# Attention and highway layer in one kernel: the weights come in as bf16 by four GpSimd DMAs

## The chip, the cores and the metric

The kernel runs on one core of a Trainium2 chip. The metric is the device time of one execution in microseconds (us), the median of three runs. The profile is of one further execution; its times count from the start of that execution's span.

TensorE (PE) multiplies matrices, VectorE (DVE), ScalarE (ACT) and GpSimd (POOL) work element by element, and SyncE (SP) here does nothing but issue DMAs. Each engine takes its instructions in one fixed order. Only PE does matrix products[...].

## The reference

The input is `q`, `k`, `v` of (4 batches, 8 heads, 768 positions, 64 columns) in float32. The attention is linear with a decay `lam` per head, in blocks of 64 positions:

```python
intra = (qb @ kb.T * Dmask) @ vb            # within the block
inter = (qb * lam**(pos+1)) @ kv_state      # what came before
out   = intra + inter
kv_state = lam**64 * kv_state + (kb * lam**(63-pos)).T @ vb
```

The result, rearranged to `x` of 3072 tokens by 512 columns, goes through a highway layer with two 512 x 512 weights:

```python
H = relu(x @ w_h);  T = sigmoid(x @ w_t + b_t)
result = T * H + (1 - T) * x                # = x + T * (H - x)
```

## The kernel before, in words

The work is cut into 12 chunks of 256 positions, three per batch. Each chunk has all 8 heads, and two halves of 128 tokens. The numbers behind a name below are the chunk and the part: `k1.0` is the first four heads of `k` of chunk 1 (chunks 0 and 1 come in two parts each, the others whole).

For each chunk:

- `load` (line 208) fetches `q`, `k`, `v` with DMAs of 256 KB on SP's queue, in rows of 512 bytes; whole chunks take two DMAs for each of the three.
- `cast_k` makes `k` bf16 (its copy runs in line 173 on ACT, 175 on DVE and POOL); `scale` (line 217) multiplies `q` and `v` by powers of `lam` and writes bf16.
- `trans` (line 223) transposes `k` and `q` on PE, and `evac_h` copies the result out of PSUM.
- `scores` (line 239), `mask` (line 243, DVE), and `intra` (line 264) are the product inside the block; `state` (line 272) adds to the running `kv` sum in PSUM, an evacuation to `ss` copies it out, and `inter` (line 252) multiplies with it. `inter` and `intra` of a chunk add up in PSUM tile `o`, which `evac_x` copies to `xT`.
- `block` (line 293) is the highway product: `ffn h g0.0` is half the columns of `xT @ w_h` for chunk 0 in eight matmuls, `ffn t g0.0` the same with `w_t`. `hmx` (297), `sigm` (306) and `thmx` (309) make the elementwise part; `turn` (315) transposes back and adds; `evac_o` copies out; `store` (line 324) writes to memory on SP's queue.

Line 198 is `fill`: matmuls of an identity at the start whose results nobody uses, which keep PE busy while the first data comes.

The weights: `load_w` (line 169) issues eight DMAs of 256 KB on SP, each of half the rows and half the columns of one weight, in rows of 1 KB, into float32 tiles `w_f`. Eight casts (`cw`) then make bf16 tiles `w_b`: four on POOL, three on ACT, one on DVE. `wh.y0` below stands for the first 256 columns of `w_h`, `wt.y1` for the last 256 of `w_t`.

The order is not left to a scheduler. Every step is a task with a number. The list `ORDER` says in which order tasks are emitted, and so the order of each engine's queue, the SP queue of DMAs among them. The strings in `EN` say which engine takes a task that could run on several (`A` for ACT, `V` for DVE, `G` for POOL). Waits between engines follow from the tiles that are read and written.

The start, decoded from `ORDER` (fills left out):

```
SP   v0.0 k0.0 q0.0 q0.1 k0.1 v0.1 q1.0 k1.0 k1.1 q1.1 v1.0 v1.1 q2 k2 v2
     wt.y1 (2 DMAs) wh.y0 (2) wh.y1 (2) wt.y0 (2) q3 k3 v3 ...
POOL scale v0.1, q1.0; cast k1.0; scale q1.1, q2, v2;
     cast wh.y0, wh.y1, wt.y0 (2); th g0.1 ...
PE   trans k0.0 q0.0 q0.1 k0.1, scores 0.0 0.1, trans k1.0 q1.0, intra 0, state 0.0, inter 0,
     state 0.1, scores 1.0, trans q1.1, state 1.0, trans k1.1, state 1.1, inter 1, scores 1.1,
     trans k2, trans q2, intra 1, scores 2.0, state 2.0, ffn t g0.1, ffn t g1.1,
     inter 2, scores 2.1, ffn h g0.0, ...
```

Of the kernel before, what the change touches and what calls it, by code (L numbers as in the profile page):

```python
# [8 lines left out]
F32 = mybir.dt.float32  # L9
# [11 lines left out]
class Task:  # L21
# [9 lines left out]


LETTER = dict(A="ACT", V="DVE", G="POOL")
KINDS = {"SP": "lw l l2 st st1 st3", "DVE": "m hx hx1 hx4 thD thD1 thD4 btc", "POOL": "thP thP1 thP4", "ACT": "g g1 g4 pow tab", "PE": "bt fill tr tr2 kv i i0 s a f f1 f4 x x1 x3"}
FIXED = {kind: eng for eng, kinds in KINDS.items() for kind in kinds.split()}
LA = 5
XB = 3
# [4 lines left out]
TH = ["DVE", "POOL"]  # L42
GROUPS = [[0], [1], [2], [3], [4], [5], [6], [7], [8], [9], [10]]
EN = dict(
    cw="GVGGGAAA", ck2="VVGA", cq2="VVGG", cv2="VGVV", et2="VAAVAVAV", ss="AAVAAAAVAVAAAAVVAVAV", xT="VAVAAAAAAAAAAAAAAAAAAAAA",
    eo="AVVAAAVAAVAVAVAAAAVAVA", ck="VAAGGAGVGG", cq="GVGGGGGGGG", cv="GGGGGGGGGG", et="AVAVAVVAVAAAAAAAAAAA", eo1="A", eo3="AA")
ORDER = [
    34, 32, 20, 33, 21, 43, 22, 42, 23, 16, 44, 24, 25, 26, 83, 27, 35, 17, 28, 82, 37, 29, 30, 36, 92, 31, 46, 38, 40, 93, 39,
    41, 84, 45, 50, 48, 51, 47, 52, 94, 49, 53, 86, 55, 133, 54, 56, 85, 132, 57, 88, 95, 134, 90, 18, 89, 58, 91, 96, 12, 59, 19,
    64, 60, 63, 87, 61, 107, 65, 100, 97, 14, 62, 108, 102, 98, 109, 99, 136, 103, 0, 101, 104, 105, 106, 110, 135, 2, 111, 138,  # L50
    8, 140, 112, 139, 10, 137, 141, 113, 6, 13, 4, 114, 15, 145, 142, 171, 146, 115, 1, 73, 147, 143, 170, 123, 3, 74, 172, 9,
    144, 211, 124, 148, 66, 149, 7, 11, 150, 71, 5, 210, 67, 68, 72, 116, 174, 69, 212, 151, 121, 70, 152, 117, 75, 251, 173, 178,
    122, 118, 153, 179, 176, 175, 119, 250, 154, 177, 120, 79, 76, 155, 214, 252, 185, 77, 80, 180, 161, 181, 186, 184, 213, 187,
    125, 289, 188, 182, 218, 189, 162, 156, 190, 183, 215, 219, 288, 216, 157, 159, 217, 158, 191, 254, 290, 160, 220, 192, 225,
    126, 221, 193, 226, 129, 253, 201, 227, 328, 127, 130, 258, 163, 256, 202, 194, 329, 257, 255, 259, 224, 195, 228, 263, 222,
    330, 229, 196, 292, 223, 230, 260, 264, 197, 231, 370, 164, 261, 291, 232, 265, 167, 233, 199, 198, 165, 293, 369, 262, 168,
    200, 266, 294, 267, 296, 331, 203, 295, 234, 407, 297, 236, 268, 332, 235, 298, 368, 237, 269, 303, 334, 299, 238, 270, 241,
    333, 304, 406, 271, 239, 305, 335, 336, 240, 242, 373, 204, 408, 300, 205, 337, 302, 306, 272, 307, 301, 243, 448, 308, 207,
    338, 273, 372, 208, 343, 309, 344, 339, 447, 277, 310, 345, 311, 274, 410, 278, 446, 279, 275, 244, 371, 280, 276, 319, 487,
    245, 409, 342, 320, 346, 281, 340, 374, 347, 341, 488, 376, 348, 411, 375, 317, 377, 312, 486, 412, 313, 247, 413, 349, 318,  # L60
    450, 81, 378, 248, 381, 350, 314, 379, 351, 382, 414, 449, 315, 206, 383, 352, 415, 451, 316, 282, 380, 353, 283, 249, 384,
    452, 385, 321, 454, 453, 386, 285, 416, 284, 490, 286, 387, 455, 169, 421, 417, 354, 422, 388, 287, 389, 423, 357, 489, 246,
    355, 128, 359, 491, 358, 209, 390, 356, 360, 78, 494, 391, 166, 361, 420, 495, 424, 131, 418, 322, 425, 419, 397, 426, 325,
    323, 492, 398, 326, 324, 362, 427, 327, 493, 456, 461, 395, 457, 428, 462, 429, 365, 463, 363, 460, 396, 366, 364, 464, 458,
    465, 499, 367, 392, 459, 466, 435, 500, 393, 501, 430, 394, 496, 431, 399, 467, 432, 436, 468, 497, 469, 437, 433, 498, 438,
    434, 502, 400, 503, 439, 472, 401, 504, 470, 402, 473, 403, 471, 505, 404, 474, 440, 506, 405, 477, 441, 520, 475, 442, 478,
    507, 476, 443, 509, 508, 479, 444, 512, 510, 521, 445, 513, 514, 511, 523, 522, 515, 480, 483, 524, 516, 481, 528, 484, 526,
    525, 482, 529, 531, 485, 527, 517, 532, 530, 518, 533, 534, 519, 535, 536]


@with_exitstack
def kernel(
# [11 lines left out]
    nc = tc.nc  # L84
# [4 lines left out]
    DM = H * D  # L89
    KC = DM // 128  # L90
# [4 lines left out]
    singles = ctx.enter_context(tc.tile_pool(name="singles", bufs=1))  # L95
# [32 lines left out]
    id_f = singles.tile([KC, KC], F32)  # L128
    nc.vector.tensor_copy(id_f, id128[0:KC, 0:KC])
    bt_col = singles.tile([128, KC], F32)  # L130
    w_f = [singles.tile([128, KC, DM], F32, name=f"w_f{i}") for i in range(2)]
    w_b = [singles.tile([128, KC, DM], BF16, name=f"w_b{i}") for i in range(2)]
    wh, wt = w_b

# [16 lines left out]
    def task(kind, emit, reads=(), writes=(), after=(), only=()):  # L151
        eng = FIXED.get(kind)
        if eng is None:
            i = count.get(kind, 0)
            count[kind] = i + 1
            eng = LETTER[EN[kind][i]]
        t = Task(kind, eng, emit, [made[x] for x in reads], [made[x] for x in writes], after, only)
        tasks.append(t)
        return t

    V, A, P, T = nc.vector, nc.scalar, nc.gpsimd, nc.tensor
    ENG = {"DVE": V, "POOL": P}


    def piece(x, y, i):
        return x[:, 2 * i:2 * i + 2, y * 256:(y + 1) * 256]

    def load_w(w, y, i):
        nc.sync.dma_start(out=piece(w_f[w], y, i), in_=piece((moe_w_h, moe_w_t)[w].rearrange("(kc p) n -> p kc n", p=128), y, i))

    def copy(eng, dst, src):
        if eng == "ACT":
            A.activation(dst, src, AF.Copy)  # L173
        else:
            ENG[eng].tensor_copy(dst, src)  # L175

    w_done = {}
    for y, w in ((0, 0), (0, 1), (1, 0), (1, 1)):
        w_done[w, y] = []
        for i in range(2):  # L180
            a = task("lw", lambda eng, w=w, y=y, i=i: load_w(w, y, i))
            w_done[w, y].append(task("cw", lambda eng, w=w, y=y, i=i: copy(eng, piece(w_b[w], y, i), piece(w_f[w], y, i)), after=[a]))


    def powers(eng):
# [98 lines left out]
    def group(n, b):  # L284
        for g in GROUPS:
            if n in g:
                return g[0], 2 * (n - g[0]) + b, 2 * len(g)
        return n + b, 0, 1
# [39 lines left out]
    for n in range(N):  # L328
        bt, c = divmod(n, NST)
        P2 = n < PARTS  # L330
        parts = [slice(0, 4), slice(4, 8)] if P2 else [slice(0, 8)]
        y = "2" if P2 else ""
# [58 lines left out]
        for b in range(2):  # L391
            g, r, z = group(n, b)
            y = {1: "1", 2: "", 4: "4"}[z]
# [9 lines left out]
            w = 1 if z == 4 else 2  # L403
# [24 lines left out]
            y = "3" if fin else "1"  # L428
# [45 lines left out]
```

## Time and profile before

| | |
|---|---|
| time, median of 3 runs | 113.19 us (113.16 to 113.62) |
| span of the profiled execution | 110.9 us |
| PE busy | 101.5 us (92%) |
| DVE, ACT, POOL busy | 78.4, 72.9, 63.5 us |
| DMA | 27.57 MB, 20.98 MB read and 6.29 MB written in main memory, 249 GB/s over the span |
| casts of the weights | 4 on POOL of 614 ns, 3 on ACT of 623 ns, 1 on DVE of 416 ns |

How to read it: the page gives the busy share of each engine in 40 slices of the span (one slice is 2.8 us here), a digit for each, nine for 90% or more. `PEclk` is PE's granted clock in tenths of full speed. The chain is the work that ended last, followed back step by step to what released each. A line such as "20.64 1.90 PE w L223 x16" is a start, a length, an engine, the tile written, the source line and the number of instructions.

### The profile page before, as it was taken

How to read it: one execution, taken by the hardware profiler on the slowest of the kernel's cores; microseconds unless marked ns; L12 is line 12 of the kernel's file. 1: busy time of each engine (PE TensorE's matmuls, PEld its weight loads, DVE VectorE, ACT ScalarE, POOL GpSimd, SP SyncE). 2: the span in 40 equal slices, each digit the busy share in tenths (PEclk: the TensorE clock that was granted, in tenths of full speed). 3: DMA queues.
4: the chain of work that ended last, by engine and by line, in shares of the span. 5: the costliest groups of instructions: out<-in, count | busy, mean ns of one | idle time of the engine just before them, and what ended most of it. 6: DMA issues, size and time to landing. Idle time of an engine off the chain costs nothing.

```text
span 110.9 us, 4776 instructions
## 1 busy us (share of the span) xinstructions
PE 101.5 (92%) x2073; PEld 86.3 (78%) x2073; DVE 78.4 (71%) x128; ACT 72.9 (66%) x137; POOL 63.5 (57%) x55
## 2 busy tenths in 40 slices
PE   4996489689999999999999999999999999999960
PEld 1353469578889889888888889999899888889950
DVE  0179896684998899797778854788775797764630
ACT  3574443177288967668695788787878844785780
POOL 6004626263469899988979979899940040401420
PEclk9999965559999999999999999999999999999998
DMA  0999999999999999999999999999995250024263
GB/s 10 267 292 290 290 293 287 293 356 320 253 290 297 288 292 292 290 294 289 293 287 287 279 292 295 292 264 370 392 343 204 107 188 0 6 101 183 101 236 142
DMA packets 43964, 27.57 MB, mean 249 GB/s; under 512 B 1828, under 2 KB 41000, under 8 KB 43944
## 3 DMA queue, kind: packets, MB, share of 16 engines
q1 hardware_dynamic: 43792, 27.27, 88.3%
q8 instruction: 16, 0.26, 1.0%
q14 instruction: 4, 0.03, 0.1%
q10 hardware_dynamic: 152, 0.01, 0.1%
HBM read 20.98 MB, written 6.29 MB: 246 GB/s over the span
## 4 chain that ended last, share of the span: by engine, by line
PE 76%; SPq 11%; DMA 6%; DVE 2%; issue 1%; POOLq 1%; ACT 0%; DVEq 0%
PE w L293 39%; SPq L208 11%; PE w L315 10%; PE w L223 10%; DMA kf<-in_k_dram 6%; PE w L239 5%; PE o L264 5%; PE kv L272 4%; PE o L252 4%; DVE qT L175 1%; POOLq L469 1%; DVE kb L175 1%; DVE hmx L297 0%; ACT o_sb L173 0%; DVEq L175 0%
## 5 line engine op out<-in xcount | busy, mean ns | idle before, releaser
L293 PE MATMUL w<-xT,w_b 128*128 128x256 bf16 (+1 forms) x416 | 46.9, 265 | 0.0
L293 PEld LDWEIGHTS <-w_b 128*128 128x128 bf16 x416 | 36.5, 98 | 4.4
L243 DVE TENSOR_TENSOR m<-w,tri 128x512 bf16<-128x512 f32 x48 | 30.8, 684 | 4.2 <-PE w L239 3.8
L309 POOL TENSOR_TENSOR th<-t_sb,hmx 128x512 bf16<-128x512 bf16 (+1 forms) x13 | 15.1, 1165 | 23.5 <-DVE hmx L297 14.4
L217 POOL TENSOR_TENSOR vs<-vf,pow_k 128x1024 bf16<-128x1024 f32 (+1 forms) x11 | 20.1, 1824 | 12.2 <-DMA vf<-in_v_dram 11.1
L297 DVE SCALAR_TENSOR_TENSOR hmx<-w,xT 128x512 bf16<-128x512 f32 (+1 forms) x26 | 16.5, 646 | 7.7 <-PE w L293 7.4
L217 POOL TENSOR_TENSOR qb<-qf,pow_q 128x1024 bf16<-128x1024 f32 (+1 forms) x11 | 19.2, 1746 | 4.2 <-DMA qf<-in_q_dram 4.2
L306 ACT ACTIVATE w<-w,bt_col 128x256 f32<-128x256 f32 (+1 forms) x26 | 11.2, 432 | 7.6 <-PE w L293 5.7
L173 ACT ACTIVATE xT<-o 128x512 bf16<-128x512 f32 x22 | 12.1, 597 | 3.7 <-PE o L264 2.3
L173 ACT ACTIVATE kT<-w 128x1024 bf16<-128x1024 bf16 (+1 forms) x11 | 10.0, 906 | 6.9 <-PE w L223 6.9
L315 PE MATMUL w<-id,th 128*128 128x128 bf16 x96 | 12.9, 219 | 0.6 <-POOL th L309 0.6
L239 PE MATMUL w<-qT,kT 64*64 64x128 bf16 x384 | 12.8, 231 | 0.7 <-ACT kT L173 0.3
L315 PE MATMUL w<-id,xT 128*128 128x128 bf16 x96 | 12.9, 220 | 0.0
L173 ACT ACTIVATE o_sb<-w 128x512 f32<-128x512 f32 (+1 forms) x17 | 9.6, 575 | 4.8 <-PE w L315 4.6
L306 ACT ACTIVATE t_sb<-w,bt_col 128x256 bf16<-128x256 f32 (+1 forms) x26 | 10.5, 458 | 3.0 <-PE w L293 3.0
L309 DVE TENSOR_TENSOR th<-w,hmx 128x512 bf16<-128x512 f32 (+1 forms) x13 | 8.4, 648 | 4.2 <-ACT w L306 4.0
L223 PE MATMUL w<-id,kb 128*128 128x128 bf16 x96 | 8.5, 231 | 2.8 <-DVE kb L175 1.4
L272 PE MATMUL kv<-vs,kb 64*64 64x64 bf16 x320 | 10.4, 203 | 0.1
L315 PEld LDWEIGHTS <-th 128*128 128x128 bf16 x96 | 9.4, 98 | 0.9 <-POOL th L309 0.8
L239 PEld LDWEIGHTS <-kT 64*64 64x64 bf16 x384 | 9.1, 112 | 1.2 <-ACT kT L173 0.5
L272 PEld LDWEIGHTS <-kb 64*64 64x64 bf16 x320 | 8.8, 117 | 1.3 <-issue 1.0
L315 PEld LDWEIGHTS <-xT 128*128 128x128 bf16 x96 | 9.3, 98 | 0.5
(46 smaller groups left out, 118.9 us busy)
## 6 DMA issues: line engine op xcount, KB each, us to landing
vf<-in_v_dram SPq DMA_DIRECT2D x24, 256.0 KB, 5.4
kf<-in_k_dram SPq DMA_DIRECT2D x24, 256.0 KB, 5.5
qf<-in_q_dram SPq DMA_DIRECT2D x24, 256.0 KB, 5.5
out_dram<-o_sb SPq DMA_DIRECT2D x23, 256.0 KB, 3.5
w_f<-in_moe_w_t_dram SPq DMA_DIRECT2D x4, 256.0 KB, 6.1
w_f<-in_moe_w_h_dram SPq DMA_DIRECT2D x4, 256.0 KB, 6.2
out_dram<-o_sb SPq DMA_DIRECT2D x2, 128.0 KB, 1.9
lam_bc<-in_lam_dram ACTq DMA_DIRECT2D x1, 4.0 KB, 3.5
```

What stands on the lines that cost most here:

```text
L173: A.activation(dst, src, AF.Copy)
L208: nc.sync.dma_start(out=get(x, n, p)[:, h - hs.start:h - hs.start + 4, :], in_=src[b, h:h + 4, c * 2 * C:(c + 1) * 2 * C, :].rearrange("h ...
L217: ENG[eng].tensor_tensor(dst[:, hs], in0=get(x, n, p).rearrange("p h (j d) -> p h j d", j=J), in1=pw[:, :, :, None].to_broadcast([128, hs. ...
L223: T.transpose(get(x + "tr", n, p)[:, i, j, :], get(x + "b", n)[:, j, h:h + 2, :], id128)
L239: T.matmul(get("s", n, u, e)[half(b), i, j, :], lhsT=turned("k", n)[half(e), hp, b * C + j:(b + 1) * C:J], rhs=turned("q", n)[half(e), hp, ...
L243: V.tensor_tensor(get("m", n, u)[:, e], in0=get("s", n, u, e), in1=tri[:, None].to_broadcast([128, 2, J, C]), op=ALU.mult)
L272: T.matmul(get("kv", n // NST)[half(e), hp, :], lhsT=get("kb", n)[half(b), j, 2 * hp + e, :], rhs=get("vs", n)[half(b), 2 * hp + e, j, :], ...
L293: T.matmul(get(x, g, js[0])[:, i, :], lhsT=w[:, kc, j * 128:(j + 1) * 128], rhs=get("xT", g)[:, kc, :], start=(kc == 0), stop=(kc == KC - 1))
L297: V.scalar_tensor_tensor(get("hmx", g, js[0]), in0=get("h", g, js[0]), scalar=0.0, in1=get("xT", g)[:, js[0]:js[-1] + 1, :], op0=ALU.max, ...
L306: A.activation(get(*gate(g, js))[:, i, :], get("t", g, js[0])[:, i, :], AF.Sigmoid, bias=bt_col[:, j:j + 1])
L309: ENG[TH[js[0] // len(js) % 2]].tensor_tensor(get("th", g)[:, js[0]:js[-1] + 1, :], in0=get(*gate(g, js)), in1=get("hmx", g, js[0]), op=AL ...
L315: T.matmul(get("x", n, b, p)[:, (j - js[0]) * 128:(j - js[0] + 1) * 128], lhsT=get(x, g)[:, j, r * C:(r + 1) * C], rhs=id128, start=(j == ...
```

## The change

The weights no longer come as float32. GpSimd issues four DMAs, one for each weight and half of its columns, which convert to bf16 on the way and write `w_b` directly. So the float32 tiles `w_f` and the eight casts are gone, and SP issues no weight DMA. The purpose is to take the casts off POOL, ACT and DVE, and the weight DMAs out of SP's queue. The number of tasks falls from 537 to 529, and the whole order and the engine choices are planned anew.

```diff
-KINDS = {"SP": "lw l l2 st st1 st3", ... "POOL": "thP thP1 thP4", ...
+KINDS = {"SP": "lw l l2 st st1 st3", ... "POOL": "gw thP thP1 thP4", ...
-    cw="GVGGGAAA", ck2="VVGA", cq2="VVGG", cv2="VGVV", et2="VAAVAVAV", ...
+    ck2="AVGV", cq2="GVGG", cv2="GGGG", et2="AVAAVAAA", ...
-    w_f = [singles.tile([128, KC, DM], F32, name=f"w_f{i}") for i in range(2)]
-    def piece(x, y, i):
-        return x[:, 2 * i:2 * i + 2, y * 256:(y + 1) * 256]
-
-    def load_w(w, y, i):
-        nc.sync.dma_start(out=piece(w_f[w], y, i), in_=piece((moe_w_h, moe_w_t)[w].rearrange("(kc p) n -> p kc n", p=128), y, i))
+    def load_w(w, y):
+        nc.gpsimd.dma_start(out=w_b[w][:, :, y * 256:(y + 1) * 256],
+                            in_=(moe_w_h, moe_w_t)[w].rearrange("(kc p) n -> p kc n", p=128)[:, :, y * 256:(y + 1) * 256])
-        w_done[w, y] = []
-        for i in range(2):
-            a = task("lw", lambda eng, w=w, y=y, i=i: load_w(w, y, i))
-            w_done[w, y].append(task("cw", lambda eng, w=w, y=y, i=i: copy(eng, piece(w_b[w], y, i), piece(w_f[w], y, i)), after=[a]))
+        a = task("gw", lambda eng, w=w, y=y: load_w(w, y))
+        w_done[w, y] = [task("lw", lambda eng: None, after=[a])]
```

The `lw` tasks that remain emit nothing; they only hold a place in the order. The new start, decoded from the new `ORDER` and `EN` (fills left out):

```
SP   q0.0 v0.0 v0.1 k0.0 k0.1 q0.1 q1.0 q2 k1.0 k1.1 q1.1 v1.0 v1.1 k2 v2 q3 k3 v3 ...
POOL DMA wh.y0, DMA wt.y1, DMA wt.y0, scale q0.0, v0.0, v0.1, DMA wh.y1,
     scale q1.0, q2; cast k1.0; scale q1.1, v1.0, v1.1, v2, q3; th g0.1 ...
ACT  cast k0.0 ... cast k2 ...
PE   trans q0.0 k0.0, scores 0.0, trans k0.1 q0.1 q1.0, scores 0.1, intra 0, trans q2,
     state 0.0, trans k1.0, inter 0, trans q1.1, scores 1.0, state 0.1, trans k1.1,
     state 1.0, inter 1, scores 1.1, trans k2, state 1.1, intra 1, ffn h g0.0, scores 2.0,
     state 2.0, ffn h g1.0, ffn h g0.1, inter 2, scores 2.1, ffn t g1.0, ...
```

POOL's queue begins, before and after, with the masks and index tables of the setup.

## The prediction

> **What bounds the kernel now.** I read three things in order: the slices of the page, the stretches of time, then the chain that ended last. From the page:
>
> ```profile
> PE   4996489689999999999999999999999999999960
> PEclk9999965559999999999999999999999999999998
> DMA  0999999999999999999999999999995250024263
> ```
>
> DMA is full from the second slice (2.8 us) to about 83 us; PE is full from the tenth (25 us) to the 38th. So there are two regimes, with the border near 25 us. The stretches show it in numbers (busy time of PE, PEld, DVE, ACT, POOL, then clock, DMA share, GB/s):
>
> ```profile
> 10.00:15.00 5.00, 2.72 (x101) 2.24 (x102) 4.47 (x9) 2.10 (x4) 3.48 (x4) 0.95 1.22 290
> 15.00:20.00 5.00, 4.68 (x109) 3.87 (x102) 3.25 (x7) 1.85 (x4) 1.90 (x1) 0.50 1.15 294
> 20.00:25.00 5.00, 4.04 (x82) 3.65 (x83) 4.09 (x6) 2.64 (x5) 2.40 (x2) 0.53 1.02 326
> 30.00:80.00 50.00, 50.00 (x1127) 44.25 (x1125) 40.33 (x63) 38.95 (x69) 45.43 (x29) 1.00 1.12 298
> 80.00:106.00 26.00, 26.00 (x546) 23.56 (x544) 18.08 (x31) 17.95 (x39) 5.67 (x6) 1.00 0.37 137
> ```
>
> From 30 to 106 us PE has no idle time, at full clock. DVE, ACT and POOL have slack there. Before 25 us PE has idle time and half a clock. The chain says what it waits for:
>
> ```profile
> 13.23 6.57 DMA kf<-in_k_dram
> ...
> 19.89 0.70 DVE kb L175
> ...
> 20.64 1.90 PE w L223 x16
> ...
> 22.56 1.24 DVE qT L175
> ...
> 23.84 0.63 PE w L239 x13
> 24.48 0.39 PE kv L272 x13
> 24.87 1.85 PE w L293 x16
> ```
>
> The DMA is the one of k of chunk 2, 16th of the 256 KB loads on SP, landed at 19.84. The first highway product starts at 24.87, and PE never stops again. So the time is: the moment when the unbroken stretch begins, plus PE work that is still to be done, plus a tail of some 5 us after the last products. Removing work from DVE, ACT or POOL after 25 us shortens none of the three.
>
> The casts and the arrival of the weights, on POOL:
>
> ```profile
> 21.58 1.90 POOL L217 TENSOR_TENSOR vs<-vf,pow_k 128x1024 bf16<-128x1024 f32 x1 [2.63 <-DMA vf<-in_v_dram]
> 24.51 0.61 POOL L175 CAST w_b<-w_f 128x512 bf16<-128x512 f32 x1 [1.02 <-DMA w_f<-in_moe_w_h_dram]
> 25.99 0.61 POOL L175 CAST w_b<-w_f 128x512 bf16<-128x512 f32 x1 [0.87 <-DMA w_f<-in_moe_w_h_dram]
> 27.50 1.38 POOL L175 CAST w_b<-w_f 128x512 bf16<-128x512 f32 x2 [0.89 <-DMA w_f<-in_moe_w_t_dram]
> ```
>
> Each waits for a weight DMA: the third, fifth and seventh of the eight. They are 1.49 and 1.51 us apart for two, so one 256 KB weight DMA occupies the DMA engines for 0.75 us. The v of chunk 2, last of 18 loads, landed at 21.58, before the weights. The weights arrive just in time: each cast is over before PE comes to its block, since PE shows no wait after 25 us.
>
> **What the Trainium skill says.** The page "DMA: Bandwidth & Descriptors", section "Issuing engines are not separate DMA queues", says that DMAs from all issuers run on the same 16 DMA engines and interleave. Its section "Queues, rings and completion order" says that an engine goes round robin between the rings that have work, at packet granularity. The trace before has nearly all bytes on one ring, so it does not show the sharing; it does show the engines full. The same page, "SWDGE vs HWDGE vs iDMA", says a cast in a DMA has to be issued from GpSimd, whose cores write the descriptors in software; no run here shows its cost yet. "TensorE: Matmul & The Clock Gate", section "What's actually happening", says the clock is halved after an idle window and comes back after some 3.4 us of sustained work. The trace agrees on the direction (0.50 from 15 to about 24.6 us, full after 25 us), though PE was 94% busy from 15 to 20 us and stayed at half.
>
> **The change part by part.**
>
> *Casts removed.* On POOL 4 x 0.614 = 2.5 us, ACT 3 x 0.623 = 1.9 us, DVE 0.42 us. All ran between 22.7 and 28.9 us and no PE step waited for them. Worth nothing on the path.
>
> *Weight bytes.* Main memory still gives 2.1 MB of float32; only the SBUF side halves. If reading sets the price, the DMA time is unchanged, 8 x 0.745 = 6.0 us. Bounds: half of that if written bytes counted, twice if the conversion is slow. I take 6.0.
>
> *When the weights come.* This is the part that counts. POOL's setup ends at 2.75 us with an iota, and its next three instructions are three of the four weight DMAs; the fourth follows scale v0.1. SP has then issued only some five loads, and the DMA engines are full from 2.8 us. So all 6.0 us of weights go ahead of, or between, the loads of chunks 0 to 2, where before they came behind all of them. The engines do not idle, so whichever ring goes first, the sum by the landing of k2 is 16 loads plus 8 weight units: 19.84 + 6.0 = 25.8 us. By the same count v1.1, now the 14th load instead of the 12th (q2 was moved ahead of k1), lands two loads earlier, 2 x 0.91, at 24.0. The 0.91 is from the trace: POOL and DVE stop waiting for q2 (14th) at 17.05 and for q0.1 (fourth) at 7.92.
>
> *What hangs on them.* In PE's new order the first highway product, ffn h g0.0, stands behind inter 1, scores 1.1, trans k2, state 1.1 and intra 1. Although its weights are there early, PE can't reach it sooner. From v1.1 at 24.0: scale v1.1 on POOL 1.04, to 25.1; state 1.0 0.5, to 25.6; ss on DVE 0.42, to 26.0; inter 1 0.7 and scores 1.1 0.6 at half clock, to 27.4; two masks 1.29, to 28.7; intra 1 1.07, to 29.8. From k2 at 25.8: cast on ACT 1.05, trans k2 0.9 behind scores 1.1; it fits within. At full clock the four PE steps take half, and intra 1 ends near 28.5. So ffn starts at 28.5 to 29.8 instead of 24.87: +3.7 to +4.9 us.
>
> *Work left at that point.* Before, scores 2.0 and state 2.0 were already done; now they follow: about 0.25 each at full clock, +0.5. I count 46 changes between 64-row and 128-row products on PE after the first highway product, against 42; the chain shows 0.98 against 0.87 us for eight L293 products behind such a change, so 4 x 0.11 = +0.4.
>
> *Descriptors on POOL.* The trace has none. From below take the 0.5 us that SP needs for one unhindered load; from above 3 us, as POOL's work up to scale v1.1 is 9.8 us (seven scales of 1.04, one of 1.90, one cast of 0.61), which fits before 25 us unless the three DMAs take over 9 us. Nothing on the path for anything in these bounds. The scale waits behind them are for data that lands after 5 us anyway.
>
> *The new engine choices and the steady part.* PE is the bound there, and its products are the same in number. I take zero.
>
> Sum: 113.2 + 3.7 to 4.9 + 0.5 + 0.4 gives 117.8 to 119.0. I take 117.9, the lower end, because two rings at work may raise the rate a little (the page has up to 392 GB/s in a slice, against some 290 here).
>
> **The rivals.**
>
> *The weights ride along for nothing.* For it: 290 GB/s with 512-byte rows is not the most that the page shows (392 in a slice with stores), so a second ring might use what the first leaves. Against it: the DMA engines' share is at or above 1. Then k2 lands at 19.84; its chain is cast 1.05, trans 1.0, state 0.6, intra 1.07, so ffn at 23.6, 1.2 us sooner; less 0.5 and 0.4 that is -0.3: 112.9, and 112.5 without the changes on PE. Even this best case gains little. Faster than before.
>
> *Partly hidden.* Half of the 6 us is absorbed: about 115.3.
>
> *The converting DMA is the bound.* Conversion at half rate makes 12 us of the 6, or descriptors cost 4 us or more each on POOL and push v1.1 to 28.5. k2 at 31.8 gives 113.2 + 6 + 4.9 = 124; the POOL case, 3.4 more than my forecast, 121.5.
>
> **How the numbers follow.** Forecast 0.62, partly hidden 0.14, for nothing 0.14, converting DMA or POOL the bound 0.10. The range: the for-nothing case lies between 112.5 and 113.2 and I leave out its faster half; from above I include the POOL case but not the 124. So 112.9 to 121.5. Chances: faster by over 0.5% 0.10 (the for-nothing case, and gains from the new plan that I don't see), within 0.5% 0.07, slower 0.83.
>
> **What would show it.** Right: k's cast of chunk 2 waits for its DMA until about 25 us, the first L293 product starts at 28 to 30 us, and from there PE is full to some 5 us before the end, with a stretch as long as now plus about 1 us. DMA stays full at about 300 GB/s, and the POOL casts of w_b are gone with no gain for PE. Wrong: GB/s clearly above 330 between 4 and 15 us with k2 near 20 us (for nothing), or scale q0.0 on POOL starting after 12 us with data long there (descriptors), or the first L293 product early but PE with holes after it.

## The result and the profile after

The kernel with the change takes 120.11 us (the median; 119.2 to 120.51) against 113.19 us: a ratio of 1.059, with a 95% interval of 1.052 to 1.066. It is slower, by 6.9 us; the forecast was 117.9, in a range of 112.9 to 121.5. A median counts every execution of a kernel, a ratio leaves out those that came out more than 1.5% above the kernel's fastest. The span of its profiled execution is 118.2 us, against 110.9. Line numbers are those of before less five: the highway products of L293 are L288 here, the scales of L217 are L212, the loads of L208 are L203.

The slices of the page (one is 3.0 us now), in the same three rows as before:

```profile
PE   5983226998999999999999999999999999999960
PEclk9998555555699999999999999999999999999997
DMA  0999999999999999999999999506494422022373
```

PE has a hole in the fourth to sixth slices, 9 to 18 us (3, 2, 2), where before the digits were 6, 4, 8, 9. Its clock stays at half until the eleventh slice, some 31 us, instead of 25. DMA is full from the second slice, as it was.

The stretches (busy time of PE, PEld, DVE, ACT, POOL, then clock, DMA share, GB/s):

```profile
10.00:15.00 5.00, 1.86 (x28) 1.04 (x25) 1.66 (x4) 1.19 (x2) 0.00 (x0) 0.60 1.29 231
15.00:20.00 5.00, 1.75 (x32) 1.15 (x34) 1.94 (x4) 1.19 (x2) 1.81 (x2) 0.50 1.15 279
20.00:25.00 5.00, 4.89 (x94) 3.76 (x88) 2.83 (x5) 2.04 (x3) 4.72 (x5) 0.50 1.08 284
25.00:30.00 5.00, 4.51 (x101) 3.69 (x99) 3.06 (x6) 2.42 (x5) 2.73 (x2) 0.50 1.09 288
30.00:80.00 50.00, 50.00 (x1110) 43.84 (x1105) 40.58 (x64) 35.98 (x63) 35.75 (x24) 0.99 1.04 268
80.00:113.00 33.00, 33.00 (x697) 29.48 (x696) 27.57 (x45) 21.49 (x45) 11.27 (x9) 1.00 0.41 149
```

Between 10 and 20 us PE is busy for 1.86 + 1.75 = 3.6 us; before it was 2.72 + 4.68 = 7.4. DVE has 3.6 us there, before 7.7, and POOL did nothing at all from 10 to 15 us. All three stand waiting for loads, or for a step that is queued behind a load. From 30 to 113 us PE is busy without a gap, as it was from 30 to 106. So the loss lies ahead of 31 us. The 231 GB/s of the first row are no sign of a slow bus: bytes are counted as written. The page counts 1.05 MB for GpSimd's DMAs and 26.52 MB in all (27.57 before), while main memory still reads 20.98 MB; a float32 weight that is written as bf16 counts half.

The chain that ended last, from 5 to 32 us:

```profile
5.13 10.95 DMA qf<-in_q_dram
...
16.17 1.04 POOL qb L212
17.25 0.61 PE w L218 x4
17.86 0.63 PE w L234 x11
...
19.22 1.91 POOL qb L212
21.18 1.03 PE w L218 x8
...
28.56 0.97 PE w L218 x8
29.53 0.41 PE kv L267 x6
30.09 0.92 PE o L259 x24
31.01 1.23 PE w L288 x8
```

The first wait is not the one of before, for k of chunk 2. It is the load `q1.0`, the seventh on SP, which took 10.95 us and landed at 16.1. From 21.18 us on the chain is almost wholly PE at half clock, and the first highway product starts at 31.0 us instead of 24.87. From it to the end are 118.2 - 31.0 = 87.2 us; before, 110.9 - 24.87 = 86.0. The 7.3 us between the two spans are thus 6.1 us of later start and 1.2 us more behind it.

The same on POOL's timeline, with the four new DMAs:

```profile
2.71 0.94 POOL L165 DMA_DIRECT2D w_b<-in_moe_w_h_dram  x1
3.65 1.48 POOL L165 DMA_DIRECT2D w_b<-in_moe_w_t_dram  x2
...
9.19 0.80 POOL L165 DMA_DIRECT2D w_b<-in_moe_w_h_dram  x1
16.17 1.03 POOL L212 TENSOR_TENSOR qb<-qf,pow_q 128x512 bf16<-128x512 f32 x1 [6.17 <-DMA qf<-in_q_dram]
19.22 1.90 POOL L212 TENSOR_TENSOR qb<-qf,pow_q 128x1024 bf16<-128x1024 f32 x1 [2.02 <-DVE m L238]
21.07 0.61 POOL L172 CAST kb<-kf 128x512 bf16<-128x512 f32 x1
21.73 1.04 POOL L212 TENSOR_TENSOR qb<-qf,pow_q 128x512 bf16<-128x512 f32 x1
22.73 2.04 POOL L212 TENSOR_TENSOR vs<-vf,pow_k 128x512 bf16<-128x512 f32 x2
27.27 1.90 POOL L212 TENSOR_TENSOR vs<-vf,pow_k 128x1024 bf16<-128x1024 f32 x1 [2.50 <-DMA vf<-in_v_dram]
```

One weight DMA costs POOL 0.74 to 0.94 us. `v2`, the last of the 18 loads of chunks 0 to 2, lands at 27.27 us; before it was 21.58. That is 5.7 us, close to the whole time of the weights' bytes. Most of these went ahead of `q1.0`: by 16 us GpSimd's ring (its own line of waiting DMA packets) had moved 1975 of its 2112 packets. Also to be seen: the scale of `q2` (19.22) stands ahead of the cast of `k1.0` (21.07), which chunk 1 needs first.

### The profile page after: what moved, and what is told of

Same layout as the page of the kernel before. It is cut to its first block, busy times and chain, and to the rows that moved or that the text cites. A ratio compares the mean times of both kernels' runs of the same rounds, so it can differ in the third digit from the quotient of the medians.

```text
span 118.2 us, 4773 instructions
## 1 busy us (share of the span) xinstructions
PE 104.4 (88%) x2073; PEld 87.0 (74%) x2073; DVE 79.8 (67%) x131; ACT 71.0 (60%) x128; POOL 65.0 (55%) x57
## 2 busy tenths in 40 slices
DMA packets 43900, 26.52 MB, mean 224 GB/s; under 512 B 1764, under 2 KB 40936, under 8 KB 43880
## 3 DMA queue, kind: packets, MB, share of 16 engines
q0 software_dynamic: 2112, 1.05, 6.6%
HBM read 20.98 MB, written 6.29 MB: 231 GB/s over the span
## 4 chain that ended last, share of the span: by engine, by line
PE 78%; DMA 9%; SPq 3%; POOL 2%; DVE 1%; ACT 1%; issue 1%; POOLq 1%
PE w L288 37%; PE w L218 11%; DMA qf<-in_q_dram 9%; PE w L310 9%; PE w L234 6%; PE o L259 5%; PE kv L267 5%; PE o L247 5%; SPq L203 3%; POOL qb L212 2%; POOLq L464 1%; DVE m L238 1%; ACT kT L170 1%; DVE hmx L292 0%; DVE ss L172 0%
## 5 line engine op out<-in xcount | busy, mean ns | idle before, releaser
L288 PE MATMUL w<-xT,w_b 128*128 128x256 bf16 (+1 forms) x416 | 47.6, 265 | 0.0
L288 PEld LDWEIGHTS <-w_b 128*128 128x128 bf16 x416 | 36.6, 98 | 4.7 <-issue 0.2
L304 POOL TENSOR_TENSOR th<-t_sb,hmx 128x512 bf16<-128x512 bf16 (+1 forms) x13 | 14.0, 1079 | 33.2 <-DVE hmx L292 17.4
L212 POOL TENSOR_TENSOR qb<-qf,pow_q 128x1024 bf16<-128x1024 f32 (+1 forms) x13 | 22.1, 1702 | 9.7 <-DMA qf<-in_q_dram 6.5
L212 POOL TENSOR_TENSOR vs<-vf,pow_k 128x1024 bf16<-128x1024 f32 (+1 forms) x13 | 21.2, 1636 | 5.7 <-issue 3.2
L301 ACT ACTIVATE w<-w,bt_col 128x256 f32<-128x256 f32 (+1 forms) x26 | 11.2, 432 | 10.7 <-PE w L288 5.6
L170 ACT ACTIVATE kT<-w 128x1024 bf16<-128x1024 bf16 (+1 forms) x13 | 12.0, 925 | 6.6 <-PE w L218 6.6
L170 ACT ACTIVATE xT<-o 128x512 bf16<-128x512 f32 x17 | 9.5, 598 | 8.0 <-PE o L259 6.9
L170 ACT ACTIVATE qT<-w 128x1024 bf16<-128x1024 bf16 (+1 forms) x9 | 7.9, 881 | 8.6 <-PE w L218 8.6
L218 PE MATMUL w<-id,qb 128*128 128x128 bf16 x96 | 8.7, 238 | 4.4 <-DVE qb L212 2.2
L218 PEld LDWEIGHTS <-qb 128*128 128x128 bf16 x96 | 6.7, 106 | 5.6 <-POOL qb L212 2.6
L259 PE MATMUL o<-m,vs 64*64 64x128 bf16 x384 | 9.1, 233 | 1.1 <-DVE m L238 1.1
```

The costliest lines, as they stand in the source:

```text
L212: ENG[eng].tensor_tensor(dst[:, hs], in0=get(x, n, p).rearrange("p h (j d) -> p h j d", j=J), in1=pw[:, :, :, None].to_broadcast([128, hs. ...
L218: T.transpose(get(x + "tr", n, p)[:, i, j, :], get(x + "b", n)[:, j, h:h + 2, :], id128)
L259: T.matmul(get("o", n)[half(e), b, 2 * u + i, :], lhsT=get("vs", n)[half(b), 4 * u + 2 * i + e, j, :], rhs=get("m", n, u)[half(b), e, i, j ...
L288: T.matmul(get(x, g, js[0])[:, i, :], lhsT=w[:, kc, j * 128:(j + 1) * 128], rhs=get("xT", g)[:, kc, :], start=(kc == 0), stop=(kc == KC - 1))
L301: A.activation(get(*gate(g, js))[:, i, :], get("t", g, js[0])[:, i, :], AF.Sigmoid, bias=bt_col[:, j:j + 1])
L304: ENG[TH[js[0] // len(js) % 2]].tensor_tensor(get("th", g)[:, js[0]:js[-1] + 1, :], in0=get(*gate(g, js)), in1=get("hmx", g, js[0]), op=AL ...
```

## Experiments

The theory: the 6.0 us of weight bytes go ahead of the first loads, and this alone makes the loss. The rivals: the converting DMA itself is slow, or takes POOL's time; or the new order of the tasks is at fault. The edits are moves in `ORDER`, shown as queues. An edited kernel's lines are shifted by one to six: L289, L290 and L294 below are still the highway products.

### The weights late, in the kernel after (e1_late)

```diff
 POOL
-DMA wh.y0, DMA wt.y1, DMA wt.y0, scale q0.0, v0.0, v0.1, DMA wh.y1,
-scale q1.0, q2; cast k1.0; scale q1.1, v1.0, v1.1, v2
+scale q0.0, v0.0, v0.1, q1.0, q2; cast k1.0; scale q1.1, v1.0, v1.1,
+DMA wh.y0, wh.y1, wt.y0, wt.y1, scale v2
```

> The changed kernel with its four weight DMAs moved on POOL to behind scale v1.1, in the order in which PE needs them; nothing else moved. Theory (the weights' 2.1 MB go ahead of the loads of chunks 0 to 2 and push them back by some 5.7 us): q1.0 is scaled near 11 us instead of 16.2, v2 lands near 22 us, the first highway product starts at 24 to 27 us instead of 31, and the time is 113 to 116 us. Rival A (the new order of PE and the new engine choices cost the time, whatever the DMAs do): 118 us or more. Rival B (a converting DMA issued by GpSimd is slow in itself): the weights come late here, PE waits for them in front of the first highway products, 117 us or more.

Measured: 115.14 us, ratio 1.021 (1.013 to 1.029). The first highway product, on PE's timeline:

```profile
24.99 1.80 PE L289 MATMUL w<-xT,w_b 128*128 128x256 bf16 x8
```

It is back at 24.99 us, where before it had 24.80 to 24.87, in the new order and with converting DMAs. `v2` is scaled at 21.76. So moving the four DMAs, and nothing else, takes away the late start and 5.0 of the 6.9 us. What stays lies behind the first product: 113.1 - 25.0 = 88.1 us, where before it was 86.0. One part is PE's clock: those eight products take 1.80 us at half clock, 1.05 at full (in e10 below). The chain that ended last names another, the last weight DMA, though it is small: PE's weight load waits 0.4 us for it.

```profile
20.59 11.38 DMA w_b<-in_moe_w_t_dram
31.97 0.04 issue
32.02 1.05 PE w L289 x8
```

### The weights early, without GpSimd DMAs (e2_plain_early)

The kernel before with its casts and its order, only the eight float32 weight loads on SP moved up.

```diff
 SP
-v0.0 k0.0 q0.0 q0.1 k0.1 v0.1 q1.0 k1.0 k1.1 q1.1 ... v2 wt.y1 (2) wh.y0 (2) wh.y1 (2) wt.y0 (2) q3
+v0.0 k0.0 q0.0 q0.1 k0.1 wh.y0 (2) v0.1 wt.y1 (2) q1.0 wt.y0 (2) k1.0 wh.y1 (2) k1.1 q1.1 ... v2 q3
```

> The kernel before, with its eight float32 weight loads moved forward on SP's queue between the loads of chunks 0 and 1, ahead of the second half of k of chunk 1; the casts stay. No GpSimd DMA, no new order elsewhere. Theory (bytes ahead of the chunk loads): v2 lands near 27 us instead of 21.6, the first highway product starts 4 to 6 us later, 117 to 119 us. Rival A (new order) and rival B (GpSimd DMA): neither is in this kernel, so 113 to 114 us.

Measured: 120.67 us, ratio 1.063 (1.053 to 1.072). Its chain:

```profile
19.33 6.37 DMA kf<-in_k_dram
...
25.79 0.84 DVE kb L176
...
26.68 1.90 PE w L224 x16
...
30.73 1.85 PE w L294 x16
```

Here k of chunk 2 lands at 25.70 us (it was 19.84), to a tenth the 25.8 of the prediction's count, and the first product starts at 30.7. The whole loss is there with plain DMAs from SP, and the casts still in. Neither GpSimd, nor conversion, nor the new order is needed for it. It came out a little larger than I had expected.

### What the conversion costs (e4_cast_in_place, e8_no_cast)

`e4_cast_in_place` is the kernel before with the change's DMAs and without the casts, at about the place of the old loads: behind `scale q2` on POOL. `e8_no_cast` has the same four DMAs at the same place, but into the float32 tiles, with the eight casts kept; it was timed once.

```diff
 POOL (both)
-... scale q1.1, q2, v2, ...
+... scale q1.1, q2, DMA wt.y1, DMA wh.y0, DMA wh.y1, DMA wt.y0, scale v2, ...
 load_w (e8 alone)
-nc.sync.dma_start(out=piece(w_f[w], y, i), ...)
+if i == 0:
+    nc.gpsimd.dma_start(out=w_f[w][:, :, y * 256:(y + 1) * 256], ...)
```

> The kernel before with its own order and engine choices, its SP weight loads and its casts taken out, and the four converting GpSimd DMAs put behind scale q2 on POOL (near 19 us), first the last half of the columns of w_t, as PE needs them. Theory (the casts were off the path, and the DMA by itself costs what the plain one does): 112.7 to 114.2 us, no change. Rival B (slow in itself, by descriptors or conversion): the first highway product waits for weights, 116 us or more. Rival C (the casts cost something after all): 112 us or less.

> The kernel before with its weights loaded as float32 by four GpSimd DMAs behind scale q2, where the run with converting DMAs in place has them; the eight casts stay. Read is when the weights land, not the time. Theory (a GpSimd DMA shares the DMA engines with SP's full ring, and so gets only about half of them): the last weight lands 11 to 13 us after its issue, as with conversion. Rival (the conversion is what is slow): it lands within 6 to 8 us.

Measured: 117.14 us for e4, ratio 1.035 (1.029 to 1.040), and 116.78 us for e8. "No change" was wrong for e4. PE starts the highway at 25.59 us, almost as before, and then stops twice:

```profile
25.59 1.92 PE L290 MATMUL w<-xT,w_b 128*128 128x256 bf16 x16
...
30.90 1.05 PE L290 MATMUL w<-xT,w_b 128*128 128x256 bf16 x8 [1.44 <-DMA w_b<-in_moe_w_h_dram]
33.32 1.92 PE L290 MATMUL w<-xT,w_b 128*128 128x256 bf16 x16 [1.38 <-DMA w_b<-in_moe_w_t_dram]
```

The bracket is the idle time ahead of the group and what ended it: 1.44 + 1.38 = 2.8 us without weights. From issue to landing these DMAs took 6.2, 8.9 and 11.3 us (least, median, most); SP's own weight loads, half as large, had taken 6.1 in the median. In e8 it was 6.6, 8.5 and 9.8 us, and the last weight arrived at 31.8:

```profile
31.82 1.17 POOL L178 CAST w_b<-w_f 128x512 bf16<-128x512 f32 x2 [1.16 <-DMA w_f<-in_moe_w_t_dram]
```

So the weights are late without conversion too. Between e4 and e8 lie 0.4 us of the median landing, or 1.5 of the latest, in one profile of each. That is not conversion alone: e8's packets write 4 KB each, e4's 512 bytes.

The lateness comes with the second ring. On SP the weights stood ahead of `q3` and had the DMA engines nearly to themselves, 6.0 us for all of them. From GpSimd in e4 the first packets moved between 21.5 and 22 us, over 2 us after the issue at 19.37; why so late, no run shows. From then on the weights shared the engines with SP's loads of chunk 3. The trace counts this by ring; here are packets, MB and share of the 16 engines' time from 22 to 30 us in e4, with GpSimd's ring as q0 and SP's as q1:

```profile
q0 software_dynamic: 1789, 0.89, 83.6%
q1 hardware_dynamic: 1745, 0.87, 45.7%
```

The rings take turns almost packet for packet. The 0.89 MB are counted as written; read as float32 they are 1.78, two thirds of all bytes read. That is 0.22 MB per us for the weights, where alone on SP they had 2.1 MB in 6.0 us, or 0.35.

### Casting DMAs one scale earlier (e12_cast_earlier)

```diff
 POOL (e4)
-scale q1.1, q2, DMA wt.y1, wh.y0, wh.y1, wt.y0, scale v2
+scale q1.1, DMA wt.y1, wh.y0, wh.y1, wt.y0, scale q2, v2
```

> The kernel before in its own order with converting GpSimd DMAs, now issued behind scale q1.1 (near 14.5 us) instead of behind scale q2 (19.4 us, 117.1 us, PE waiting 2.8 us for weights). Theory (a GpSimd DMA takes about half of the DMA engines from SP's ring at once, urgent or not): the weights are all there by 28 us, and k2 lands 2 to 3 us later than 19.8; what PE no longer waits for weights it waits for k2, 115 to 117.5 us. Rival (the DMA engines have room for both): k2 stays at 20 us and the time falls to 113 to 114 us.

Measured: 115.72 us, ratio 1.015 (1.007 to 1.023). The time is as expected, the wait is another one. PE no longer stops for weights. k of chunk 2 still comes at about 20 us: the first weight packets move between 17 and 18 us, over 2 us after the issue, and SP's ring is then nearly through with that load. It is `v2`, next in the ring, that moves:

```profile
23.59 1.90 POOL L214 TENSOR_TENSOR vs<-vf,pow_k 128x1024 bf16<-128x1024 f32 x1 [4.09 <-DMA vf<-in_v_dram]
```

and the state product that needs it holds PE:

```profile
25.54 0.63 PE L269 MATMUL kv<-vs,kb 64*64 64x64 bf16 x16 [1.01 <-POOL vs L214]
```

The first 16 highway products start at 26.11 us instead of 24.80, and in this profiled execution (116.59 us) they take 3.60 us at half clock, before 1.92 at full. So the wait for `v2` is not the whole of its loss.

Issue at 14.4 us delays the loads, issue at 19.4 us starves the highway. Neither is as good as the loads on SP, which stand exactly behind `v2` and ahead of `q3`.

### Was the rest of the late start the order? (e3_q2_back, e6_trans_later, e10_both_later)

The start slipped by 6.1 us where the prediction had 3.7 to 4.9. Two places in the new order stood out: POOL's `scale q2` ahead of chunk 1, and PE's queue, where `trans q1.0` (whose load lands at 16.1) stands ahead of `scores 0.1` and `intra 0`.

```diff
 e3:  SP load q2, POOL scale q2, PE trans q2 and its copy
-ahead of k1.0's
+behind v1.1's on SP and POOL, behind trans k2 on PE
 e6:  PE
-trans q1.0, scores 0.1, intra 0, trans q2, state 0.0, trans k1.0, inter 0, ...
+scores 0.1, intra 0, state 0.0, trans k1.0, inter 0, trans q1.0, ... scores 1.1, trans q2
 e10: both, with trans q2 behind trans k2
```

> The changed kernel with q of chunk 2 put back where the kernel before has it: its load behind that of v1.1, its scale behind scale v1.1, its transposition behind that of k2. The weight DMAs stay early. Theory (bytes, and on top of them PE standing at trans q2 until 21.2 us with the rest of chunks 0 and 1 behind it at half clock): PE goes on with state 0.0 and chunk 1 at 18 to 19 us, the first highway product starts 1 to 2.5 us sooner than 31 us, 117.5 to 119 us. Rival (the place of q2 matters nothing, k2 and v1.1 alone set the start): 120 us as it was. Rival A in its strong form (the place of q2 is the whole loss): 114 us.

> The changed kernel with two steps later on PE alone: trans q1.0 behind inter 0 and trans q2 behind scores 1.1 (their evacuations with them); loads and weight DMAs as in the changed kernel. Theory (what my sum left out is that trans q1.0 and trans q2, whose loads come late, hold up the rest of chunk 0 and all of chunk 1 in PE's queue, which then runs at half clock): chunk 0 is through by 18 us instead of 22, the first highway product starts at 28.5 to 30 us instead of 31, 118 to 119.3 us. Rival (the landing of v1.1 and k2 alone sets the start): 120 us as before.

> The changed kernel with both earlier edits together: q of chunk 2 back behind v1.1 (load, scale, transposition), and trans q1.0 behind inter 0. Each alone left the start of the highway products at 31 us. Theory (two queues were equally late: PE's behind trans q1.0, and POOL's, where scale q2 stood before cast k1.0; either alone hides the other): the first highway product starts at 29 to 30 us, where the cast and transposition of k2 put it, 118 to 119.3 us. Rival (the landing of k2 and v1.1 alone sets the start): 31 us and 120 us again.

Measured: e3 119.61 us, ratio 1.056 (1.049 to 1.064), first product at 30.97; the 1 to 2.5 us that I expected of it are not there. e6 120.58 us, ratio 1.064 (1.059 to 1.069), first product at 30.68. There PE stands at the cast of `k1.0`, which on POOL is still behind `scale q2`:

```profile
21.43 0.61 PE L219 MATMUL w<-id,kb 128*128 128x128 bf16 x4 [1.97 <-POOL kb L173]
```

Both together, e10, 119.29 us, ratio 1.056 (1.052 to 1.059):

```profile
29.17 1.05 PE L289 MATMUL w<-xT,w_b 128*128 128x256 bf16 x8
```

Each of the two queues hid the other, so that mending one showed nothing. Together they make 1.8 us of the late start, in one profile of each kernel. In the time no gain is shown: the medians differ by 0.8 us, but the intervals of the two ratios overlap. What is left of the late start hangs on chunk 0: e10's chain begins with the load `q0.1`, landed at 14.25, and runs from there through steps on PE, at half clock until some 28 us.

### More fill for the clock (e7_more_fill)

```diff
+for i in range(12):
+    task("fill", fill, writes=[("fill",)])
 PE: three of them behind trans q0.0, one behind trans k0.0, four behind trans k0.1, four behind trans q0.1
```

> The changed kernel with 12 more fills on PE, in the gaps from 8 to 17 us in which it waits for loads of chunk 0 and 1; nothing else is moved. Theory (PE works off chunks 0 and 1 at half clock because it had been idle, and that is 1 to 2 us of the loss): the clock stays at or near full until the first highway product, which starts 1 to 2.5 us earlier, 117.5 to 119 us. Rival (PE's clock matters nothing there, the loads set the start): 120 us.

Measured: 120.06 us, ratio 1.052 (1.043 to 1.060), first product at 31.07. The stretches:

```profile
15.00:20.00 5.00, 3.24 (x50) 1.71 (x53) 2.34 (x4) 1.19 (x2) 1.51 (x2) 1.00 1.14 273
20.00:25.00 5.00, 4.07 (x87) 3.01 (x78) 2.70 (x5) 1.91 (x3) 4.97 (x5) 0.67 1.02 278
25.00:30.00 5.00, 4.51 (x101) 3.70 (x94) 3.20 (x6) 2.41 (x5) 2.80 (x2) 0.50 1.13 297
```

The clock stays full to about 21.5 us and then falls all the same, in the stretch that decides. So this doesn't tell what the half clock costs between 22 and 31 us.

### An order that uses the early weights (e5_highway_early, e9_highway_early2)

If the weights are there early, chunk 0's highway could fill PE's hole. In the kernel after, with the DMAs behind `scale v0.1` and the load, scale and transposes of `q2` back behind chunk 1's:

```diff
 PE (e5, e9)
-... inter 0, trans q1.1, scores 1.0, ... intra 1, ffn h g0.0, scores 2.0, ...
+... inter 0, ffn h g0.0, trans q1.0, k1.0, state 0.1, scores 1.0, ffn t g0.0, ffn h g0.1,
+trans q1.1, k1.1, ffn t g0.1, ... intra 1, trans k2, ffn h g1.0, ...
 POOL (e9 against e5)
-scale v1.0, th g0.1, scale v1.1
+scale v1.0, v1.1, ... th g0.1
```

> The changed kernel with the early weights put to use: the four weight DMAs behind scale v0.1 in the order in which PE needs them, and the highway products of chunk 0 and their transposition back moved ahead of the second half of chunk 1, into the time in which PE waits for loads. q of chunk 2 is back behind v1.1, and intra 1 and chunk 1's first product come ahead of chunk 2. Theory (the loads are pushed back all the same, by some 5.7 us, and the loss was that PE had nothing that it could do meanwhile): four blocks and chunk 0's transpositions are done by 25 us, PE is full from 26 to 27 us with some 4 us less to do than the kernel before at 24.9, 111 to 114 us. Rival (early bytes cost their time whatever PE does): 117 us or more.

> The order with chunk 0's highway products early, with what held it up taken out: on POOL th g0.1 now comes behind scale v1.1 and scale q2 (it had stood before scale v1.1 and kept POOL idle from 16.6 to 26.6 us), on DVE k of chunk 1 is cast before th g0.0, and chunk 0's transposition back comes after chunk 1's first product. Theory (early weights need not cost the time if PE has work for them): state 1.0 near 24 us, PE full from 27 us on with 4 us less to do, 112 to 115 us. Rival (the loads of chunks 1 and 2 are 5.7 us later whatever is done with the weights, and PE waits for them): 117 us or more.

Measured: e5 122.26 us, ratio 1.080 (1.073 to 1.087). This was a fault of my order, not of the idea: on POOL an elementwise step of the highway stood ahead of the scale of `v1.1` and kept the queue from 16.6 to 26.6 us:

```profile
26.63 1.15 POOL L305 TENSOR_TENSOR th<-t_sb,hmx 128x512 bf16<-128x512 bf16 x1 [10.04 <-ACT t_sb L302]
```

With that mended, e9 took 120.87 us, ratio 1.059 (1.048 to 1.070), no better than the kernel after. The loads were not what held it: `v1.1` was scaled by 17.5 us. PE went from one dependent step to the next, and the first product of chunk 1 came at 31.57. An order found by hand is no proof that no order makes the early weights pay; that stays open.

### Late weights with the mended queues (e11_late_both)

```diff
 POOL (e10)
-DMA wh.y0, DMA wt.y1, DMA wt.y0, scale q0.0, v0.0, v0.1, DMA wh.y1, ... v1.1, ...
+scale q0.0, v0.0, v0.1, ... v1.1, DMA wh.y0, wh.y1, wt.y0, wt.y1, ...
```

> The same two edits, and the weight DMAs behind scale v1.1 as in the run with late weights (115.1 us). Theory: bytes out of the way and the queues cleared, the first highway product starts at 23.5 to 25 us; what is left over the kernel before is that weights come at half rate beside SP's loads, 113.5 to 115.5 us. Rival (what is left in that run is the new order of the steady part): 115 us, no change.

Measured: 115.56 us, ratio 1.019 (1.011 to 1.027), the same as e1's 1.021. Only its times are used here. With the weights out of the way the two queues cost nothing. None of the versions tried is as fast as the kernel before.

## Why the prediction was right and where it was off

**What bounds the kernel.** Right. PE has no wait from 31 us to the end of its products in the kernel after, and the time is again the start of that stretch plus what is left.

**Casts.** Right that they are worth nothing on the path: they are gone and no PE step came sooner. e4 and e8, without and with casts at the same place, are 117.14 and 116.78 us (the second timed once).

**Weight bytes and when they come.** Right. 6.0 us was the count; `v2` came 5.7 us later, and in e2, with the same bytes in the same early place on one ring, k of chunk 2 landed at 25.7 where the count said 25.8. e1 takes the bytes out of the way and the late start is gone. This is the cause, shown from both sides.

**Descriptors on POOL.** Right: 0.74 to 0.94 us each, between the bounds of 0.5 and 3, with nothing on the path.

**What hangs on them.** This is the term that was mis-sized: +3.7 to +4.9 was written, +6.1 was measured, and the first product came at 31.0, outside the 28 to 30 that I had named as a sign. The data came as counted: the scale of `v1.1` ended at 24.8 (predicted 25.1), and its load was no later than the count (in e6, with the same loads, POOL waits for it until 23.79). The step that failed is the next one. I took PE as free to take state 1.0 when its data came, at 25.1. It was not; three older steps stood ahead of it in its queue:

```profile
24.41 0.64 PE L234 MATMUL w<-qT,kT 64*64 64x128 bf16 x16
24.85 0.63 PE L267 MATMUL kv<-vs,kb 64*64 64x64 bf16 x16
25.41 0.61 PE L218 MATMUL w<-id,kb 128*128 128x128 bf16 x4
25.96 0.53 PE L267 MATMUL kv<-vs,kb 64*64 64x64 bf16 x11
```

These are scores 1.0, state 0.1, trans k1.1 and, at last, state 1.0. From there each step is about 1.1 us behind my upper count: `ss` on DVE ends at 27.1 instead of 26.0, intra 1 at 31.0 instead of 29.8. The lower count, 28.5, was for PE at full clock in these steps; the clock was at half until 31 us.

The backlog comes from the early loads. By the prediction's own rate the seventh load, `q1.0`, was due at 7.92 + 3 x 0.91 = 10.7 us, and it landed at 16.1. PE's queue stood there, at `trans q1.0`, with `scores 0.1` and `intra 0` behind it. Then POOL's `scale q2` held back `k1.0`. So PE was busy for 3.8 us less than before between 10 and 20 us, and had the work to do from 21 us on, at half clock: in the stretch from 20 to 25 us it was itself the bound, 4.89 of 5 us busy. With both queues mended (e10) the start is at 29.17. That this lies inside the predicted interval does not confirm the predicted path: `v1.1` is scaled by 23.4 us there, and the chain comes from `q0.1`. The link that I named, k of chunk 2 until 25 us, is not on the chain of the kernel after; it is on e2's.

**Work left.** +0.9 predicted (0.5 and 0.4), +1.2 measured. Some 0.2 of it is the clock, which I had not counted here: the first eight highway products took 1.29 us (the timeline of PE), 1.05 at full clock in e10. The runs do not split the rest, nor do they show apart from it what the new engine choices cost.

**The lower end, and luck.** I took 117.9 from 117.8 to 119.0, in the hope that two rings raise the rate. They did not: 5.7 of 6.0 us arrived. The measured 120.1 lies above the whole sum. It is inside the stated range only because the range went up to 121.5 for the case that POOL is held up by its DMAs, which did not happen. A start of 6.1 us in the same sum, 113.2 + 6.1 + 0.9, gives 120.2. Two slips of 0.1 to 0.2 changed nothing: 28.5 less 24.87 is 3.6, and 117.9 + 3.4 is 121.3.

**The rivals.** That the weights ride along for nothing, or are half hidden, falls with `v2` at 27.27. The converting DMA as the bound falls with e8, where the conversion is gone and the landing is nearly as late, and with e2, where the loss is there without it. Its 121.5 is near the measured time, but not by its mechanism.

## What to carry to other kernels

Where the DMA engines are full, a DMA that is issued earlier takes its bytes out of what comes first, and its cost is the time of those bytes at the first wait that hangs on the other loads. Ask what stands in line at that moment on each engine's queue: data that comes late also holds up the work queued behind its first user. Moving a transfer to another issuer takes it out of the order of the old queue, and here that order, weights behind `v2` and ahead of `q3`, was worth more than eight casts that were hidden anyway.

## What the runs showed of the hardware that was not expected

- **The second ring's share.** With both rings full, packets of the two went through in turn: 1789 of GpSimd's and 1745 of SP's from 22 to 30 us in e4, 654 and 646 from 9 to 12 us in the kernel after. A casting packet reads 1 KB and writes 512 bytes, a packet of SP's moves 512, so the weights had two thirds of the bytes read. In e8, with packets of 4 KB, it was 548 to 1285 packets and 2.01 to 0.64 MB, so not one to one, but three quarters of the bytes. Equal turns fit the Trainium skill, "DMA: Bandwidth & Descriptors", section "Queues, rings and completion order", which has an engine go round robin between its rings, packet by packet. What I had not drawn from it is that this holds in both directions: late weights are slowed by loads that nobody needs yet. They took 6.2 to 11.3 us from issue to landing (e4).
- **Conversion on the way** from float32 to bf16 is nearly free here. With it, and with 512-byte packets in place of 4 KB, the median landing was 0.4 us later than the 8.5 without it, and the latest 1.5 later than 9.8.
- **PE's clock** does not follow the share of time in which PE is busy. In e7 it was at full speed from 15 to 20 us with PE busy for 3.24 of 5 us, and at half from 25 to 30 us with 4.51. In the kernel after it stayed at half through a stretch with 4.89 of 5. The Trainium skill, "TensorE: Matmul & The Clock Gate", "What's actually happening", gives some 3.4 us of sustained work; these stretches do not agree, and the runs do not say what decides.
- **A cast on DVE** of 128x512 took 1.09 us, from 23.97 to 25.06, beside POOL's scales; other DVE casts of this size take 0.42. The Trainium skill, "SBUF — State Buffer", section "SBUF: two separate sides", describes a port pair that DVE and GpSimd lock against each other. The number fits it; no run tested it.
